# Attention scores in 64x64 tiles without the fully masked blocks, and one chunk's token transposes by DMA

## The chip, the cores and the metric

The kernel runs on one core of one Trainium2 chip. A core has a matrix engine (TensorE, "PE" in the profile; its weight loads are listed apart as "PEld"), VectorE ("DVE"), ScalarE ("ACT"), GpSimd ("POOL"), a queue engine (SyncE, "SP") and 16 DMA engines. The metric is the device time of one execution in microseconds (us); lower is better. A measurement is a median of several runs.

## What is computed

Attention with a sliding window of 128 keys and 4 "sink" keys that every query sees, 4 batches, 8 heads, 768 tokens, 64 numbers a head, and behind it a layer norm and a two-layer network on each token (512 to 2048 to 512), with the attention's output added at the end. Inputs and output are float32; the kernel works in bf16 inside.

```python
scores = (1.0 / np.sqrt(D)) * np.matmul(q, k.transpose(0, 1, 3, 2))
rel = pos[:, None] - pos[None, :]
keep = (pos[None, :] < n_sink) | ((rel >= 0) & (rel < window))     # n_sink 4, window 128
a = softmax(np.where(keep, scores, -1e9))
x = heads_joined(np.matmul(a, v))                                  # 4 x 768 x 512
xn = (x - mean(x)) / np.sqrt(var(x) + 1e-6) * g_ln
out = x + np.maximum(xn @ w_ch1, 0.0) @ w_ch2
```

With blocks of 128 keys and 128 queries, a query block needs two key blocks: its own, of which the half with key not after query is kept, and the one before, of which the half with key after (query − 128) is kept. Each of the two therefore has one 64x64 corner in which nothing is kept.

## The kernel before

**Tiles and chunks.** The 24 tiles of 128 tokens are worked on in 12 chunks of 256 tokens, three to a batch. `R` is a chunk's place in its batch (0, 1, 2). Chunks 0 and 1 have code of their own (`attend_tile`); chunks 2 to 11 go through `attend`. Of these, 2, 4, 5, 7, 8, 10 and 11 have R > 0, so they also use the previous chunk's keys and the sinks; 3, 6 and 9 begin a batch.

**The planner.** Nothing is written out in order by hand. Each piece of work is given to a planner with `P.op(name, engines and assumed durations, due time, function that issues it, buffers read and written)`. The planner (`Plan.run`, L113 to L195) goes through assumed time, places on each engine the ready piece with the lowest due time among those that could start within a short window (0.3 us on TensorE), gives out buffers from rings (L397 to L420; `pair` has two PSUM slots of two banks, `one` four of one bank, `vn` seven, `ot` four), and so fixes the order of instructions on every engine and queue. A `mode` marks which tile shape TensorE uses; a change of mode is assumed to cost `SWITCH`, 0.095 us. From a due time of 40 (`strict`) on, TensorE's pieces are taken in order of due time alone (L129). `PAR` (L229) holds due times and switches. The due times of chunk `c` count from `16c − 8` (`at`, L536); the two-layer network of chunk `c` has due times from `16c + 8`.

**One chunk of `attend`, and lines to know.**

- Loads are issued on GpSimd's queue: L562 (values, `vn`), L575 or L651 (keys and queries). Chunks up to 3 have keys and queries transposed on TensorE (L637), later ones by a DMA transpose on SP's queue (the call is in the helper at L551; started at L652, after the previous chunk's scores).
- Scores, in two halves of four heads: `sc`, L742 to L757. A half has two pair tiles, one for two heads. K is 64, so the array is used as two row tiles, one head in each (`h2`), each with 128 keys as stationary columns. With R > 0 there are three parts of 128, 256 and 128 queries. In the first half the four sink matmuls follow (L756).
- The exponential (L766, ScalarE) and the product with the 0/1 mask (L770, VectorE) run over the whole pair tile, 1024 columns.
- `value` (L782): the sinks' part (L789) and the window's part (L794) on TensorE for each of the two tiles, then reciprocal, product and statistics on VectorE (L807 to L815), a power on GpSimd (L821, L822), the normalised tokens `xc` on VectorE (L824), and their transposition into `xnt` (below).
- The two-layer network, `mlp`: L862 (chunks 0, 1) or L869 (later) is the first layer, evicted at L879; the second layer is L900 for chunks 0 and 1, and for later chunks a scheme with seven products in place of eight at L949 (with L932, L963, L970 on VectorE). The output is stored by SP (L912, L998).

**The transposition of tokens.** It has two forms, and `x_by_dma` says from which chunk on the first is used:

```python
        if c >= PAR["x_by_dma"]:
            P.op(f"trx{t}", {"SP": (1.2, 1.2)}, d + 0.5, lambda e: dma_t(xnt_b[c].t[:, :, 128 * i:128 * i + 128], xc.t),
                 reads=[xc], writes=[xnt_b[c]], dma=HW_X)
            return
        d = at(c, "trx") + 1.0 * i if c >= 2 else d + 0.2
        P.op(f"trx{t}", pe(0.224), d, tr, reads=[xc, Bc["ident"]], writes=[pt],
             hold=[xnt_b[c]])
```

In the second form four transposes on TensorE (L832) write a PSUM bank, and ScalarE or VectorE copies it to `xnt` (the helper's L568 for chunk 2). The first layer of a chunk from 2 on reads both tiles of `xnt` at once.

Of the kernel before, what the change touches and what calls it, by code (L numbers as in the profile page):

```python
# [64 lines left out]
class Plan:  # L65
# [47 lines left out]
    def run(self):  # L113
# [8 lines left out]
        while ready:  # L122
# [5 lines left out]
            for o in ready:  # L128
                if "PE" in o.engs and o is not head and o.prio >= PAR["strict"]:  # L129
                    continue  # L130
# [67 lines left out]
def pe(us):  # L198
    return {"PE": (us, us + Plan.PE_DRAIN)}


def act(n):
    t = 0.065 + 0.000833 * n
    return (t, t + 0.105)


def dve(n, per=1.04):
    t = 0.067 + 0.001 * per * n
    return (t, t + 0.09)


def fix(occ, extra=0.09):
    return (occ, occ + extra)
# [12 lines left out]
NEG = -1e30  # L226
NEVER = -1e9

PAR = dict(strict=40.0, win=0.4, tr=-8.0, sc=-5.3, sc1=-2.0, av=2.0, trx=9.0, by_dma=4, x_by_dma=3, g_on_w=2, behind=5, gtt=9.0, ramp=0.3, vs0=2.6, vpb=12.0,  # L229
           w1p=(0.15, 1.7, 2.05, 2.8), pm=2, w2p=(4.5, 4.51, 4.52, 4.53), by_tile=2, wino=2, vp=(0.0, 0.1, 2.0, 2.1, 4.2, 4.3), ld1=0.05)  # L230


# [129 lines left out]
def kernel(  # L362
# [12 lines left out]
    nc = tc.nc  # L375
# [19 lines left out]
    P = Plan()  # L395
# [56 lines left out]
    def constant(name, eng, us, prio, emit, reads=(), **kw):  # L452
        return P.op(name, {eng: fix(us)}, prio, emit, reads=[Bc[r] for r in reads], **kw)
# [37 lines left out]
    def negs(e):  # L491
# [14 lines left out]
    constant("ones_f", "DVE", 0.06, 7.0, lambda e: V.memset(ones_f, 1.0), writes=[Bc["ones_f"]])  # L506
    constant("masks", "DVE", 0.8, 6.0 if PAR["pm"] == 4 else -20.0, masks, ["upper"], writes=[Bc["mask"]], nb=20.0 if PAR["pm"] == 4 else 0.0)

# [3 lines left out]
    P.op("gtt", pe(0.06), 0.62, lambda e: nc.tensor.transpose(pg.t[:, 0:NDM], g4, ident_f[0:NDM, 0:NDM]),  # L512
         reads=[Bc["g4"], Bc["ident_f"]], writes=[pg], nb=PAR["gtt"])
    P.op("gt", {"DVE": fix(0.08)}, 0.63, lambda e: V.tensor_copy(gt, pg.t[:, 0:NDM]), reads=[pg], writes=[Bc["gt"]])
# [10 lines left out]

    w1prio = PAR["w1p"]
    for c in range(4):
# [3 lines left out]
    for c in range(4):  # L531
        P.op(f"w2ld{c}", {"POOL": (0.75, 0.8)}, PAR["w2p"][c], lambda e, c=c: G.dma_start(
            w2[c], moe_w_ch2[512 * c:512 * (c + 1), :].rearrange("(t p) n -> p t n", p=128)),
            writes=[Bw2[c]], dma=SW_W)

    def at(c, step):  # L536
        return 16.0 * c - 8.0 + PAR[step]

# [5 lines left out]
    tile_of, scores = {}, {}  # L544
# [185 lines left out]
    def attend(c):  # L730
        b, R = c // RC, c % RC
        kq = kq_b[c]
        kprev = kq_b[c - 1] if R else None
        n = 512 if R else 384
        ps, pp_s = (Buf(f"ps{c}", "ps"), Buf(f"pss{c}", "one")) if R else (None, None)
        pes = []
        for half in range(2):
            d = at(c, "sc1" if half else "sc")
            pps = [Buf(f"s{c}{2 * half + i}", "pair") for i in range(2)]
            pbs = [Buf(f"p{c}{2 * half + i}", "pe") for i in range(2)]  # L740

            def sc(e, pps=pps, half=half):  # L742
                if R:
                    parts = [(kprev, 128, 0, 128, 0), (kq, 0, 0, 256, 128), (kq, 128, 128, 256, 384)]
                else:
                    parts = [(kq, 0, 0, 256, 0), (kq, 128, 128, 256, 256)]
                for j, pp in enumerate(pps):
                    hp = 2 * half + j
                    for i, (kt, k0, q0, q1, col) in enumerate(parts):
                        for h2 in range(2):  # L750
                            rs = slice(64 * h2, 64 * h2 + 64)
                            nc.tensor.matmul(pp.t[:, h2, col:col + q1 - q0], lhsT=kt.t[rs, hp, 0, k0:k0 + 128],  # L752
                                             rhs=kq.t[rs, hp, 1, q0:q1], start=i == 0, stop=True, skip_group_check=True)
                if R and half == 0:
                    for hp in range(HP):
                        nc.tensor.matmul(pp_s.t[32 * hp:32 * hp + 32, 0:256], lhsT=kts_b[b].t[:, hp, :],  # L756
                                         rhs=kq.t[:, hp, 1, :], start=True, stop=True, skip_group_check=True)  # L757
            sinks = R and half == 0
            scores[c] = P.op(f"sc{c}{half}", pe(2 * n / 2400 + (0.21 if sinks else 0)), d, sc,
                 reads=[kq] + ([kprev] if R else [])  # L760
                 + ([kts_b[b]] if sinks else []), writes=pps + ([pp_s] if sinks else []),
                 hold=pbs + ([ps] if sinks else []), mode=("r", "c") if sinks else "r")
            for j, pp in enumerate(pps):
                hp = 2 * half + j
                pb = pbs[j]
                P.op(f"ex{c}{hp}", {"ACT": act(2 * n)}, d + 0.1 + 0.05 * j, lambda e, pp=pp, pb=pb: nc.scalar.activation(  # L766
                    pb.t[:, :, 0:n], pp.t[:, :, 0:n], AF.Exp, scale=scale), reads=[pp], writes=[pb])
                mm = (mask if R else mask0).rearrange("p a b c -> p a (b c)")
                P.op(f"mk{c}{hp}", {"DVE": dve(2 * n, 0.52)}, d + 0.2 + 0.05 * j, lambda e, pb=pb, mm=mm:
                     V.tensor_mul(pb.t[:, :, 0:n], pb.t[:, :, 0:n], mm),  # L770
                     reads=[Bc["mask" if R else "mask0"]], rw=[pb])
                pes.append(pb)
            if sinks:
                P.op(f"sx{c}", {"ACT": act(256)}, d + 0.6, lambda e: nc.scalar.activation(
                    ps.t, pp_s.t[:, 0:256], AF.Exp, scale=scale), reads=[pp_s], writes=[ps])
        for i in range(2):
            def part(h, n, i=i):
                col = 256 * i + 128 * n if R else 128 * (i + n)
                return pes[h // 2].t[:, h % 2, col:col + 128]
            value(c, i, pes, ps, at(c, "av") + 1.0 * i, part, [2 * c + i - 1, 2 * c + i] if R or i else [2 * c])  # L780

    def value(c, i, pes, ps, d, part, srcs):  # L782
        b, R, t = c // RC, c % RC, 2 * c + i
# [218 lines left out]
    for c in range(NC):  # L1002
        chunk(c)
        if c < 2:
            if c:
                first_sinks()
            attend_tile(2 * c)
            attend_tile(2 * c + 1)
        else:
            attend(c)  # L1010
# [34 lines left out]
    for o in order:  # L1045
# [7 lines left out]
        if free and left > 0.11:  # L1053
            i, nth = min(free)[1], 0
# [55 lines left out]
```

## Time and profile before

| | us |
|---|---|
| median of 3 runs | 215.95 (215.31 to 216.34) |
| the profiled execution | 215.84 |
| its span, first to last instruction | 214.3 |
| granted TensorE clock | 0.994 of full |

A few groups from the list of costliest ones (busy us; mean ns of one):

| line, engine | what | count | busy | mean |
|---|---|---|---|---|
| L869 PE | first layer, 128x256 | 640 | 74.5 | 273 |
| L752 PE | scores, 64x256 of 64*128 tiles | 80 | 9.6 | 271 |
| L752 PE | scores, 64x128 of 64*128 tiles | 80 and 56 | 8.4 and 6.3 | 216 and 221 |
| L756 PE | sinks, 128*32 tiles | 28 | 2.0 | 283 |
| L794 PE | values, 128x65 | 352 | 14.6 | 193 |
| L832 PE | token transposes | 24 | 2.3 | 220 |
| L766 ACT | exponential, 1024 columns | 28 | 27.1 | 1023 |
| L770 DVE | mask product, 1024 columns | 28 | 18.6 | 683 |
| L551 SPq | DMA transposes into `kq` / `xnt` | 32 / 18 | | 1228 / 1190 (median, issue) |

How to read it: a span is cut into 40 slices of 5.36 us, and a digit is the busy share in tenths. "Busy" of a group joins overlapping instructions. In a timeline a line is "start, length, engine, line, operation, out<-in, shape, count"; neighbours of one kind are merged, and brackets tell idle time before it with what ended it. The chain of waits goes back from the last instruction, at each step to what released it.

### The profile page before, as it was taken

How to read it: one execution, taken by the hardware profiler on the slowest of the kernel's cores; microseconds unless marked ns; L12 is line 12 of the kernel's file. 1: busy time of each engine (PE TensorE's matmuls, PEld its weight loads, DVE VectorE, ACT ScalarE, POOL GpSimd, SP SyncE). 2: the span in 40 equal slices, each digit the busy share in tenths (PEclk: the TensorE clock that was granted, in tenths of full speed). 3: DMA queues.
4: the chain of work that ended last, by engine and by line, in shares of the span. 5: the costliest groups of instructions: out<-in, count | busy, mean ns of one | idle time of the engine just before them, and what ended most of it. 6: DMA issues, size and time to landing. Idle time of an engine off the chain costs nothing.

```text
span 214.3 us, 5912 instructions
## 1 busy us (share of the span) xinstructions
PE 205.9 (96%) x2375; PEld 168.3 (79%) x2381; DVE 162.2 (76%) x408; ACT 115.3 (54%) x173; POOL 83.7 (39%) x126
## 2 busy tenths in 40 slices
PE   6999999999999999999999999999999999999990
PEld 2568995683787987987987987988988988988880
DVE  5689769898587688697786796797787777794470
ACT  2488579457565555554457357355555555532600
POOL 7966583449057066066075174174110110110000
PEclk9999999999999999999999999999999999999997
DMA  6999999999979939929969939939931520222003
GB/s 111 154 198 187 198 191 207 186 199 131 170 129 134 164 96 125 213 62 133 165 110 158 196 50 157 193 46 161 191 75 38 140 49 11 90 49 90 13 22 91
DMA packets 99914, 27.23 MB, mean 127 GB/s; under 512 B 88356, under 2 KB 97064, under 8 KB 99880
## 3 DMA queue, kind: packets, MB, share of 16 engines
q0 software_dynamic: 67712, 13.37, 78.5%
q1 hardware_dynamic: 31640, 13.15, 31.8%
q8 instruction: 20, 0.33, 0.7%
q10 hardware_dynamic: 528, 0.26, 0.5%
q14 instruction: 14, 0.11, 0.2%
HBM read 27.30 MB, written 6.29 MB: 157 GB/s over the span
## 4 chain that ended last, share of the span: by engine, by line
PE 83%; DMA 7%; POOL 5%; DVE 2%; issue 1%; DVEq 0%
PE one L869 33%; PE one L949 29%; DMA w<-in_moe_w_ch_dram 7%; PE one L900 6%; PE pair L752 5%; PE pair L794 4%; PE one L862 3%; POOL vn L562 2%; PE pair L789 1%; POOL nat L597 1%; PE one L756 1%; POOL st L822 1%; POOL n4b L575 1%; DVE st L813 1%; PE one L637 0%
## 5 line engine op out<-in xcount | busy, mean ns | idle before, releaser
L879 ACT ACTIVATE hq<-one 128x512 bf16<-128x512 f32 x94 | 56.1, 599 | 56.3 <-PE one L869 46.9
L869 PE MATMUL one<-xnt,w 128*128 128x256 bf16 x640 | 74.5, 273 | 0.0
L869 PEld LDWEIGHTS <-w 128*128 128x128 bf16 x640 | 61.4, 98 | 7.0
L766 ACT ACTIVATE pe<-pair 128x1024 bf16<-128x1024 f32 (+1 forms) x40 | 36.2, 960 | 23.9 <-PE pair L752 23.9
L821 POOL TENSOR_SCALAR st<-st 128x1 f32<-128x1 f32 x24 | 6.3, 262 | 88.2 <-DVE rec L807 74.0
L949 PEld LDWEIGHTS <-hs 128*128 128x128 bf16 x320 | 30.0, 98 | 5.6 <-issue 1.3
L963 DVE TENSOR_TENSOR tm<-one,x 128x256 f32<-128x256 f32 x40 | 16.9, 422 | 13.4 <-PE one L949 13.4
L770 DVE TENSOR_TENSOR pe<-pe,mask 128x1024 bf16<-128x1024 bf16 (+1 forms) x40 | 25.0, 643 | 1.6 <-ACT pe L766 1.4
L949 PEld LDWEIGHTS <-hq 128*128 128x128 bf16 x240 | 23.4, 98 | 2.7
L562 POOL DMA_DIRECT2D vn<-in_v_dram x24 | 21.8, 922 | 3.0 <-DMA w<-in_moe_w_ch_dram 1.6
L932 DVE TENSOR_TENSOR hs<-hq 128x512 bf16<-128x512 bf16 x40 | 15.4, 413 | 5.1 <-ACT hq L879 5.1
L949 PE MATMUL one<-w,hq 128*128 128x256 bf16 x160 | 19.1, 273 | 0.0
L970 DVE TENSOR_TENSOR ot<-one,tm 128x256 f32<-128x256 f32 x40 | 16.7, 417 | 1.3 <-PE one L949 1.1
L809 DVE TENSOR_TENSOR x<-pair,rec 128x512 bf16<-128x512 f32 x24 | 16.6, 691 | 0.8
L813 DVE BATCH_NORM_STATS2 st<-x 128x6 f32<-128x512 bf16 x24 | 16.6, 691 | 0.4
L862 PE MATMUL one<-xnt,w 128*128 128x128 bf16 x256 | 15.9, 219 | 0.2 <-DMA w<-in_moe_w_ch_dram 0.2
L651 POOL DMA_DIRECT2D nat<-in_k_dram x16 | 14.9, 930 | 2.4 <-DMA w<-in_moe_w_ch_dram 2.4
L651 POOL DMA_DIRECT2D nat<-in_q_dram x16 | 14.1, 896 | 3.9 <-DMA w<-in_moe_w_ch_dram 3.9
L862 PEld LDWEIGHTS <-w 128*128 128x128 bf16 x256 | 14.5, 98 | 1.0 <-DMA w<-in_moe_w_ch_dram 0.3
L822 POOL TENSOR_TENSOR st<-st,mhalf 128x1 f32<-128x1 f32 x24 | 14.5, 604 | 2.0
L900 PE MATMUL one<-w,hq 128*128 128x512 bf16 x60 | 15.0, 380 | 0.2
L794 PE MATMUL pair<-vn,pe 128*128 128x65 bf16 x352 | 14.6, 193 | 0.0
(113 smaller groups left out, 249.4 us busy)
## 6 DMA issues: line engine op xcount, KB each, us to landing
out_dram<-ot SPq DMA_DIRECT2D x22, 256.0 KB
w<-in_moe_w_ch_dram POOLq DMA_DIRECT2D x8, 512.0 KB, 12.8
vn<-in_v_dram POOLq DMA_DIRECT2D x24, 128.0 KB, 7.1
nat<-in_k_dram POOLq DMA_DIRECT2D x17, 128.0 KB, 5.1
nat<-in_q_dram POOLq DMA_DIRECT2D x17, 128.0 KB, 6.3
kq<-nat SPq DMA_TRANSPOSE x32
out_dram<-ot SPq DMA_DIRECT2D x4, 128.0 KB
xnt<-xc SPq DMA_TRANSPOSE x18
```

What stands on the lines that cost most here:

```text
L562: P.op(f"vld{t}", {"POOL": (0.87, 0.9)}, prio, lambda e: G.dma_start(bv.t[:, :, 0:64], v[b, :, 128 * r:128 * (r + 1), :].rearrange("h p d ...
L651: lambda e, nat=nat, ap=ap: G.dma_start(nat.t, ap), writes=[nat], dma=SW, after=behind(c))
L766: P.op(f"ex{c}{hp}", {"ACT": act(2 * n)}, d + 0.1 + 0.05 * j, lambda e, pp=pp, pb=pb: nc.scalar.activation(pb.t[:, :, 0:n], pp.t[:, :, 0:n ...
L770: V.tensor_mul(pb.t[:, :, 0:n], pb.t[:, :, 0:n], mm),
L794: nc.tensor.matmul(po.t[:, h // 4, 65 * (h % 4):65 * (h % 4) + 65], lhsT=part(h, n), rhs=vn_b[tv].t[:, h, :], start=(not R and h % 4 == 0 ...
L813: P.op(f"bn{t}", {"DVE": fix(0.60)}, d + 0.12, lambda e: V.bn_stats(st.t[:, 8:14], x.t), reads=[x], writes=[st, mv])
L862: nc.tensor.matmul(ph.t[:, 128 * s:128 * s + 128], lhsT=w1[u // 2][:, j, 128 * s:128 * s + 128], rhs=xnt.t[:, j, 128 * (u % 2):128 * (u % ...
L869: nc.tensor.matmul(ph.t[:, 256 * s:256 * s + 256], lhsT=w1[ht // 4][:, j, 128 * (ht % 4):128 * (ht % 4 + 1)], rhs=xnt.t[:, j, :], start=j ...
L879: nc.scalar.activation(hg.t[:, u % 4, :], ph.t, AF.Relu)
L900: nc.tensor.matmul(pc.t[:, 0:wd], lhsT=(hq[s // 2].t[:, (2 * s + i) % 4, 128 * ii:128 * ii + 128] if by_tile else hq[ht // 8].t[:, ht // 2 ...
L949: nc.tensor.matmul(at(r), lhsT=get(left, g)[:, v, s, :], rhs=rhs, start=first and n == 0, stop=n == 7, skip_group_check=True)
L963: return P.op(f"tm{name}_{c}", {"DVE": dve(256, 1.14)}, pr, lambda e: V.tensor_tensor(tm[name].t, at(r), xs[i].t[:, sl], op=ALU.add), read ...
```

## The change

1. `sc` with R > 0: each matmul is split over the key columns into two of 64 (`m`), so that a stationary operand is 64x64 and four tiles are in use (two heads by two halves of the keys). `cut` gives for each part and each half of the keys the query columns that are computed: of the previous block the first 64 keys meet only the first 64 queries, and so on. The 64x64 blocks that the mask clears entirely are not written; the exponential and the mask product still run over all columns, with what the slot held before in those blocks. A half has 24 matmuls instead of 12.
2. The planner's assumed duration of such a half falls from 2·512 to 2·384 columns, and it is marked with a mode of its own, "q".
3. `x_by_dma` 3 becomes 2: chunk 2's tokens go by DMA transposes.
4. The due time of `value` for chunk 2 goes from 26 and 27 to 20 and 21 (`av2`; `avi`, 1.0, stands for the constant that was there).

```diff
-PAR = dict(strict=40.0, win=0.4, tr=-8.0, sc=-5.3, sc1=-2.0, av=2.0, trx=9.0, by_dma=4, x_by_dma=3, g_on_w=2, behind=5, gtt=9.0, ramp=0.3, vs0=2.6, vpb=12.0,
+PAR = dict(strict=40.0, win=0.4, tr=-8.0, sc=-5.3, sc1=-2.0, av=2.0, trx=9.0, by_dma=4, x_by_dma=2, g_on_w=2, av2=20.0, avi=1.0, behind=5, gtt=9.0, ramp=0.3, vs0=2.6, vpb=12.0,
...
                     parts = [(kprev, 128, 0, 128, 0), (kq, 0, 0, 256, 128), (kq, 128, 128, 256, 384)]
+                    cut = [((0, 64), (0, 128)), ((0, 192), (64, 256)), ((0, 128), (64, 128))]
...
-                        for h2 in range(2):
-                            rs = slice(64 * h2, 64 * h2 + 64)
-                            nc.tensor.matmul(pp.t[:, h2, col:col + q1 - q0], lhsT=kt.t[rs, hp, 0, k0:k0 + 128],
-                                             rhs=kq.t[rs, hp, 1, q0:q1], start=i == 0, stop=True, skip_group_check=True)
+                        for m in range(2 if R else 1):
+                            n0, n1 = (cut[i][m] if R else (0, q1 - q0))
+                            for h2 in range(2):
+                                rs, ks = slice(64 * h2, 64 * h2 + 64), slice(64 * m, 64 * m + 64) if R else slice(0, 128)
+                                nc.tensor.matmul(pp.t[ks, h2, col + n0:col + n1], lhsT=kt.t[rs, hp, 0, k0 + ks.start:k0 + ks.stop],
+                                                 rhs=kq.t[rs, hp, 1, q0 + n0:q0 + n1], start=i == 0, stop=True, skip_group_check=True)
...
-            scores[c] = P.op(f"sc{c}{half}", pe(2 * n / 2400 + (0.21 if sinks else 0)), d, sc,
+            scores[c] = P.op(f"sc{c}{half}", pe(2 * (384 if R else n) / 2400 + (0.21 if sinks else 0)), d, sc,
...
-                 hold=pbs + ([ps] if sinks else []), mode=("r", "c") if sinks else "r")
+                 hold=pbs + ([ps] if sinks else []), mode=("q", "c") if sinks else "q" if R else "r")
...
-            value(c, i, pes, ps, at(c, "av") + 1.0 * i, part, [2 * c + i - 1, 2 * c + i] if R or i else [2 * c])
+            value(c, i, pes, ps, (PAR["av2"] if c == 2 else at(c, "av")) + PAR["avi"] * i, part, [2 * c + i - 1, 2 * c + i] if R or i else [2 * c])
```

## The prediction

> **What bounds the kernel now.** I read the page first (busy time, the slices), then the chain of waits, then TensorE's timeline around the stages that the change touches, then the shapes, last the DMA transposes.
>
> ```profile
> PE 205.9 (96%) x2375; PEld 168.3 (79%) x2381; DVE 162.2 (76%) x408; ACT 115.3 (54%) x173; POOL 83.7 (39%) x126
> PE   6999999999999999999999999999999999999990
> DMA  6999999999979939929969939939931520222003
> ```
>
> TensorE is busy in tenths of 9 from the second slice to the last but one; no other engine is. The DMA engines are as full up to about 60 us, and from then on have gaps (slices of 3 and 2), so loads catch up. The chain of waits says the same: weights from DMA until 26 us, then TensorE, with one detour over VectorE and GpSimd that ends in `xc` and L832:
>
> ```profile
> 10.91 15.07 DMA w<-in_moe_w_ch_dram
> ...
> 48.57 0.42 DVE xc L824
> 49.04 0.40 PE one L832 x4
> ...
> 65.17 0.55 PE pair L752 x12
> ```
>
> So a microsecond of TensorE's own time saved after 26 us is a microsecond of the end, unless a new wait eats it. The two pieces to price are the score stage (L752) and the transposes of chunk 2 (L832). TensorE's timeline of both, with two stages that serve as rows below:
>
> ```profile
> 45.50 1.08 PE L637 MATMUL one<-ident,n4a 128*64 128x128 bf16 x32
> ...
> 47.39 0.39 PE L832 MATMUL one<-ident,xc 128*128 128x128 bf16 x4
> 47.61 1.03 PE L900 MATMUL one<-w,hq 128*128 128x512 bf16 x4
> 49.04 0.40 PE L832 MATMUL one<-ident,xc 128*128 128x128 bf16 x4 [0.40 <-DVE xc L824]
> ...
> 65.11 0.23 PE L752 MATMUL pair<-kq,kq 64*128 64x128 bf16 x2
> 65.17 0.33 PE L752 MATMUL pair<-kq 64*128 64x256 bf16 x4
> 65.34 0.22 PE L752 MATMUL pair<-kq,kq 64*128 64x128 bf16 x2
> 65.39 0.33 PE L752 MATMUL pair<-kq 64*128 64x256 bf16 x4
> 65.65 0.29 PE L756 MATMUL one<-kq,kts 128*32 128x256 bf16 x4
> ...
> 72.88 0.65 PE L794 MATMUL pair<-vn,pe 128*128 128x65 bf16 x16
> ```
>
> The first number is the start. A matmul's duration holds its drain, which lies beside the next matmul; what counts is the distance of starts.
>
> **Scores (14 half-chunks: chunks 2, 4, 5, 7, 8, 10, 11, two halves each).** Now: 12 matmuls in a half, two row tiles at once, each streaming 128+256+128 = 512 columns for each of two pair tiles. The second pair tile starts 65.34 − 65.11 = 0.23 us after the first, and the sink matmuls start 0.31 after that, 0.09 of it the switch to another tile shape (the same 0.1 lies before 65.11: the last matmul there starts at 64.90 and streams 0.11). So a pair tile is 0.22 us, 0.43 ns a column. After: 24 matmuls of 64x64, four tiles at once, each tile 64+192+128 or 128+192+64 = 384 columns. At 0.43 ns that is 0.165 us a pair tile; the upper bound of the gain is 0.055 a pair tile, 0.11 a half, 14 × 0.11 = 1.54 us.
>
> What the trace doesn't show is a 64x64 tile, and how long its weight load holds up a matmul of only 64 columns (28 ns). The nearest rows are the matmuls of L637 and L794 above, and their weight loads among the shapes (busy us, mean ns):
>
> ```profile
> L794 PEld LDWEIGHTS <-pe 128*128 128x128 bf16 x352 | 13.8, 97 | 0.8
> ...
> L637 PEld LDWEIGHTS <-n4a 128*64 128x64 bf16 x32 | 0.9, 110 | 0.1
> ```
>
> L637 runs two column tiles with loads of 64 columns: 32 matmuls in 1.08 − 0.22 (one drain) = 0.86 us, 27 ns each, so 54–55 a tile for 128 columns at 0.43 ns (55). The load is hidden, hence at most 54 ns. L794 is the short one: 16 matmuls of 65 columns in 0.65 − 0.19 = 0.46 us, 31 ns where streaming needs 28: its load of 128 columns takes at most 31. The 64-column load of L637 is recorded 110 − 97 = 13 ns longer, so I take 31 + 12 = 43 ns, nearer to L637 because its shape is. Then each pair tile has one matmul of 64 columns in each column half that lasts 43 instead of 28: 0.165 + 0.015 = 0.18 us. Gain 0.04 a pair tile, 0.08 a half; the first load of a stage is bare and 110 − 94 = 16 ns longer than now (L752's loads have a mean of 94), which leaves 0.065. 14 × 0.065 = **0.9 us**. With loads of 54 ns it is 14 × (2 × 0.029 − 0.016) = 0.6; with hidden ones 1.5; if loads don't hide at all, a loss (rivals). The Trainium skill (TensorEngine Tiling (Array Packing), Restrictions and Gotchas) says column tiling switches the fast weight load off, and TensorE: Matmul & The Clock Gate (LDWEIGHTS) puts a load's ns at its columns divided by 1.2, an estimate of 53 ns for 64. By that figure the scores would give 0.6 us; L637's 54 ns agrees with it and can't tell it from mine.
>
> The number of switches stays: row tiles, in the first half then column tiles for the sinks, become 64x64 tiles, then column tiles. The exponentials and mask products (L766 at 1023 ns, L770 at 683 ns) still run over 1024 columns, the unwritten blocks too, so ScalarE and VectorE gain nothing.
>
> **Transposes of chunk 2.** Removed from TensorE: two groups of four at L832, each 0.22 us of starts (47.39 to 47.61, 49.04 to 49.27), 0.44 together. Also gone is the second group's wait: the four L900 before it start at 47.61 and take 4 × 0.216 = 0.86, so TensorE could have gone on at 48.47 and did at 49.04: 0.57 us lost. Sum **1.0 us**. ScalarE loses two evictions of 0.59 us (L568, 48.6 and 50.3), off the path.
>
> Added: two DMA transposes on SP's queue, 1.19 us each to issue, in front of the store at 52.5 and the key/query transposes from 53.0; SP does nothing between 44.4 and 52.5, so this costs nothing while they are issued there. Their landing I take from the semaphore events: the sixteenth comes 2.4 to 6.6 us after the issue, 6.6 for the one at 53.0 us, when the DMA engines are full as they are here. If `xc` of the second tile came at 48.99 as now, the landing would be 55.6, and the first-layer matmuls (L869, now 55.54, then about 54.4) would wait 1.2 us.
>
> That is what moving `value` of chunk 2 covers. Its two stages (L789 and L794) start at 40.48 and 42.91. Their last operand, the fourth masked tile, is ready at 39.05 (L770). With the lower due time they go in when the running group of L900 ends, about 39.6 and 40.3, 2.6 us earlier for the second tile. Behind them move VectorE's L807 to L824 and GpSimd's L821/L822 (GpSimd's queue then is loads that wait for the DMA's turn, up to 2.2 us), giving `xc` near 46.4 and a landing by 53.0: 1.4 us of slack. The work passed over (the rest of chunks 0 and 1) is later by 1.4 us, and so are stores, for which nothing waits with four `ot` buffers; TensorE's sum is the same. Two more transposes are at most 1.4 us each of all DMA engines (q1's 31.8% of 214.3 us over its fifty transposes, its stores counted in), so the next keys and queries (last landing 62.9, needed at 65.1) come up to 2.8 us later on full engines, with 2.2 of cover; part of it goes into the gaps before 65 us, and I charge nothing.
>
> **Sum.** −0.9 − 1.0 = −1.9 us against the profiled execution's 215.84 (span 214.3): 213.9. The median of the runs, 215.95, is 0.1 above that execution, so I forecast **214.0**, span 212.4.
>
> **Rivals.**
> Scores give nothing. If four tiles get no further than two, because loads of 54 ns and bare first loads add up, only the transposes pay: 214.9. For it: no 64x64 row; against: two-way packing works both by rows and by columns. 0.12.
>
> Tokens late. DMA contention or a blocked GpSimd queue holds `xc` or its landing, and the first layer of chunk 2, or the scores of chunk 4, wait up to 1.2 us: 215.2. For it: the longest landing is 6.6 us and slack 1.4. 0.10.
>
> Slower: loads don't lie beside matmuls of the same rows. Its place is L752, where two column tiles share each row half. Then each of the three rounds of a pair tile costs its longest matmul plus a load: 55 + 82 + 55 + 3 × 43 = 321 ns against 220; +0.2 a half, 14 × 0.2 = +2.8, less 1.0: 217.7. It decides from 9 ns of bare load a round, where a pair tile is back at 220 (192 + 3 × 9); from 21 ns the 28 pair tiles cost the 1.0 us of the transposes as well. Against it: L637's tiles share all rows and would need 55 + 43 = 98 ns, not 54. 0.09. The Trainium skill's page TensorE: Matmul & The Clock Gate (Packing small matmuls, The mechanism) states just this, that a load overlaps only matmuls of another row group. L637 disagrees, at 27 ns a matmul.
>
> Slower: instruction rate. The fastest long row hands out a load and a matmul every 27 ns (L637); the new stage wants 24 pairs in 0.34 us, 14 ns each. Bound at 27 it takes 0.65 instead of 0.44: +2.9 − 1.0, 217.9. Against: L756's four start within 0.29 − 0.283 = 7 ns of each other, and the long matmuls before let instructions queue up. 0.07.
>
> **Numbers.** The forecast has 0.62, mostly 213.3 to 214.6. The range 213.2 to 216.0 takes in the hidden-load bound, nothing from scores, and late tokens; it leaves out the two slower ones. A measurement here tells about 0.5% (1.08 us) from no change. Faster than 214.87: nearly all of the forecast, half of the first rival, a little of the second: 0.68. Within: 0.16. Slower: 0.16.
>
> **What would show it.** L752 with 64*64 tiles, 24 starts in about 0.37 us (chain pieces of 0.47 instead of 0.55; 0.55 or more means a slower rival); L832 x16, no wait on `xc` on TensorE; 20 transposes into `xnt`; the first L869 near 54.4. I am wrong if that L869 has a wait on DMA before it, if L752's loads show gaps, or if TensorE stalls between 40 and 50 us for banks that late evictions hold.

## The result, and the profile after

The changed kernel takes 213.95 us (median of 11 runs, 213.37 to 214.69); the kernel before, run beside it, 215.64 (11 runs, 215.15 to 216.36). The ratio is 0.9914, 95% interval 0.9897 to 0.9932: 1.7 us faster by the medians, 1.5 to 2.2 by the interval, beyond the 0.5% that such a measurement can tell. The forecast was 214.0. The profiled execution took 213.8 with a span of 212.2, where 212.4 was expected.

All lines of the new kernel from the score stage on are three higher (L752 is L755, L869 is L872). The page of the kernel after, busy times and slices:

```profile
PE 204.2 (96%) x2535; PEld 168.1 (79%) x2541; DVE 161.6 (76%) x408; ACT 114.5 (54%) x171; POOL 83.4 (39%) x126
PE   6999999999999999999999999999999999999990
DMA  5999999999999959939979959969934421122002
```

TensorE has 160 matmuls more (168 of the scores, less 8 transposes) and is busy 1.7 us less; ScalarE has two evictions less. TensorE is still what bounds the kernel. The chain of waits of the kernel after, in the stretch where the detour over `xc` was (start, length, work):

```profile
49.05 0.44 PE pair L755 x8
49.49 2.70 PE one L903 x12
52.18 0.44 PE pair L755 x8
52.62 1.83 PE one L903 x8
54.45 1.75 PE one L872 x16
...
63.93 0.46 PE pair L755 x24
64.39 0.22 PE one L759 x4
```

There is no step over VectorE or GpSimd left between 44 and 54 us, and a half of the scores is 0.46 where it was 0.55. TensorE's timeline of the same kernel, and two lines of SP's queue:

```profile
39.38 0.39 PE L792 MATMUL pair<-vs,ps 128*128 128x260 bf16 x2
...
40.09 0.39 PE L792 MATMUL pair<-vs,ps 128*128 128x260 bf16 x2
...
63.86 0.25 PE L755 MATMUL pair<-kq,kq 64*64 64x64 bf16 x4
63.91 0.31 PE L755 MATMUL pair<-kq 64*64 64x192 bf16 x8
64.05 0.23 PE L755 MATMUL pair<-kq,kq 64*64 64x64 bf16 x4
64.08 0.31 PE L755 MATMUL pair<-kq 64*64 64x192 bf16 x8
64.32 0.29 PE L759 MATMUL one<-kq,kts 128*32 128x256 bf16 x4
```

```profile
43.68 0.38 SPq L915 DMA_DIRECT2D out_dram<-ot  x1
44.18 3.43 SPq L551 DMA_TRANSPOSE xnt<-xc  x2
```

What to see: `value` of chunk 2 went in at 39.38 and 40.09 (40.48 and 42.91 before). A pair tile of scores lasts 64.05 − 63.86 = 0.19 us, the second 64.32 − 64.05 − 0.09 (the switch) = 0.18; by the same reading they were 0.23 and 0.22. The two token transposes are issued at 44.18 and 46.41 and land, by the semaphore events, at 52.06 and 53.33; the first L872 starts at 54.29.

### The profile page after: what moved, and what is told of

Its sections match the earlier page's. It is cut to its first block, busy times and chain, and to the rows that moved or that the text cites. A ratio compares the mean times of both kernels' runs of the same rounds, so it can differ in the third digit from the quotient of the medians.

```text
span 212.2 us, 6233 instructions
## 1 busy us (share of the span) xinstructions
PE 204.2 (96%) x2535; PEld 168.1 (79%) x2541; DVE 161.6 (76%) x408; ACT 114.5 (54%) x171; POOL 83.4 (39%) x126
## 4 chain that ended last, share of the span: by engine, by line
PE 95%; DVE 2%; issue 0%; DVEq 0%
PE one L872 33%; PE one L952 30%; PE one L865 7%; PE one L903 7%; PE pair L797 5%; PE pair L755 4%; PE pair L792 2%; PE one L1069 2%; PE one L637 2%; PE pair L1069 1%; PE pair L693 1%; PE one L759 1%; PE pair L705 1%; PE one L835 1%; DVE st L816 0%
## 5 line engine op out<-in xcount | busy, mean ns | idle before, releaser
L872 PE MATMUL one<-xnt,w 128*128 128x256 bf16 x640 | 74.5, 273 | 0.0
L872 PEld LDWEIGHTS <-w 128*128 128x128 bf16 x640 | 61.4, 98 | 7.1
```

Of the source, the lines that this page charges most:

```text
L872: nc.tensor.matmul(ph.t[:, 256 * s:256 * s + 256], lhsT=w1[ht // 4][:, j, 128 * (ht % 4):128 * (ht % 4 + 1)], rhs=xnt.t[:, j, :], start=j ...
```

## The experiments

Two figures are given for each kernel. One is the time with its ratio to the kernel before, run beside it. The other comes from the one profiled execution: the stretch from TensorE's first score matmul of chunk 2 (32.02 us in the kernel after) to the first one of chunk 11's second half (176.50). That first matmul lies anywhere from 31.6 to 33.0 us in the fourteen traces, whatever the kernel, a spread of over half of what the change gains. In the three latest (again, full_columns, pieces_of_64) the chain of waits lies on the weights' loads until about 27 us. The stretch leaves this out. It holds 13 of the 14 halves.

| kernel | median us | ratio (95%) | stretch us | against before |
|---|---|---|---|---|
| before | 215.64 to 215.85 | 1 | 146.62 | |
| after | 213.95 | 0.9914 (0.9897–0.9932) | 144.48 | −2.14 |
| again (after) | 213.95 | 0.9919 (0.9897–0.9940) | 144.48 | −2.14 |
| scores_only | 214.89 | 0.9953 (0.9934–0.9972) | 145.49 | −1.13 |
| tokens_only | 215.13 | 0.9969 (0.9953–0.9986) | 145.61 | −1.01 |
| move_only | 214.97 | 0.9958 (0.9943–0.9973) | 146.05 | −0.57 |
| scores_move | 213.92 | 0.9920 (0.9899–0.9941) | 144.93 | −1.69 |
| no_move | 213.80 | 0.9902 (0.9885–0.9919) | 144.75 | −1.87 |
| full_columns | 215.05 | 0.9963 (0.9948–0.9979) | 145.84 | −0.78 |
| pieces_of_64 | 215.12 | 0.9969 (0.9946–0.9992) | 145.56 | −1.06 |
| eighths | 214.25 | 0.9931 (0.9906–0.9957) | 145.13 | −1.49 |
| loads_held | 214.13 | 0.9927 (0.9907–0.9947) | 144.48 | −2.14 |
| loads_held_no_move | 213.61 | 0.9900 (0.9878–0.9921) | 144.48 | −2.14 |
| loads_behind_next | 214.80 | 0.9952 (0.9933–0.9971) | 145.79 | −0.83 |

> The changed kernel as it is, once more, beside the next three on the same chip: 213.95, ratio 0.991. Its transposes of chunk 2's second tile land 0.5 to 1 us before the first L872 can start, or after it: in the traces of three other kernels with the same tokens (no_move, pieces_of_64, eighths) that L872 waited 0.26, 0.43 and 0.56 us, in three more it didn't.

Time and ratio came out the same, and two executions of the changed kernel have the same stretch to 0.01 us. So differences of 0.1 in it are read here, though each stretch is that of one execution; the times tell apart some 0.4. (The second transpose landed at 54.27 in this one, 0.8 us before the first L872.)

### Which part brings what

```diff
 scores_only (to after)
-x_by_dma=2   av2=20.0
+x_by_dma=3   av2=26.0
```

> Only the score stage is changed (64x64 tiles, blocks left out); tokens of chunk 2 by TensorE and the old due times, as before. Theory A (TensorE's starts add up): each of the 14 halves goes from 0.545/0.548 us to 0.462/0.464, 14 x 0.083 = 1.17 us, so 215.64 - 1.17 = 214.5 (ratio 0.9946), and the wait of about 0.57 us on xc before the second L832 group stays. Rival B (the gain of the whole is the tokens' and the planner's new order; scores give nothing at the end): 215.6.

Stretch −1.13, time 214.89, and the halves take 0.462 and 0.464 us to the next start, each 0.083 less than before. Rival B falls. The wait that theory A said would stay is there (TensorE's timeline of scores_only):

```profile
48.57 0.40 PE L835 MATMUL one<-ident,xc 128*128 128x128 bf16 x4 [0.39 <-DVE xc L827]
```

```diff
 tokens_only (to before)
-x_by_dma=3   ... at(c, "av") + 1.0 * i
+x_by_dma=2   ... (20.0 if c == 2 else at(c, "av")) + 1.0 * i
```

> Old score stage; chunk 2's tokens by DMA and its values at the earlier due time. Theory A: 0.44 us of transposes and 0.57 of wait are gone from TensorE, the first L869 starts about 54.5 us instead of 55.54, 215.64 - 1.0 = 214.6 (ratio 0.9953). With scores_only it must add up to the whole, 1.17 + 1.0 = 2.2. Rival B: 214.0, all of the gain is here. Rival C (part of the gain needs both): 215.1 or more.

Stretch −1.01, as theory A has it, and −1.13 − 1.01 = −2.14 is the whole: in the stretches the parts add up, and neither needs the other. The first L869 started at 54.27. The time, 215.13 (−0.3 to −1.0 by its interval), lies at the weak end and is as a number what rival C named. But by the ratios the two parts bring −1.0 and −0.7 us and the whole −1.9, each to about ±0.4, so the times don't show that anything is missing.

```diff
 move_only (to before)
-at(c, "av") + 1.0 * i
+(20.0 if c == 2 else at(c, "av")) + 1.0 * i
```

> Old score stage, tokens by TensorE as before; only the due time of chunk 2's values is lowered to 20 and 21. Theory A: xc of the second tile is ready some 2.5 us earlier, so the wait of 0.57 us before the second L832 group is gone, 215.64 - 0.57 = 215.1, and the 0.44 of the transposes stays. Rival: the wait is only exchanged for another one behind the passed-over evictions, 215.6.

Stretch −0.57: the earlier due time alone takes the wait away, and between this stretch and that of tokens_only the transposes on TensorE are the other 0.44. The second group of transposes no longer has idle time before it:

```profile
48.20 0.39 PE L832 MATMUL one<-ident,xc 128*128 128x128 bf16 x4
```

The times don't show the 0.44: 214.97 here, 215.13 with the DMA transposes too.

### Was the earlier due time needed?

```diff
 no_move (to after)
-av2=20.0
+av2=26.0
```

> The changed kernel with the old due times (26 and 27) for chunk 2's values. Theory A: xc of the second tile is ready near 48.6 us and its DMA transpose lands 6 to 8 us later, 55 to 56.5, while the first L872 could start at 54.3: it waits 0.7 to 2 us, 213.95 + 0.7 to 2 = 214.7 to 216. Rival (landing isn't the limit, the move was not needed): no wait before that L872, 213.95.

A miss for theory A's size, and the time is the rival's. The second transpose was issued at 49.32 and landed at 54.66, 5.3 us later, and the first L872 started at 54.71, by starts 0.26 us late; the time is no worse than the changed kernel's. Issued 2.9 us earlier, the transpose lands only 1.3 us earlier (53.33). So the landing doesn't follow the issue. The next kernels ask what the early due time is worth, and whether it is DMA traffic that holds the landing.

```diff
 scores_move (to after)
-x_by_dma=2
+x_by_dma=3
```

> New score stage and the earlier due time, but chunk 2's tokens by TensorE. Theory A (TensorE's starts add up): 0.44 us of transposes are back and no wait, so 213.95 + 0.44 = 214.4. Theory H (in many executions the first L872 waits for the DMA transposes about as long as those on TensorE take): the same as the changed kernel, 213.95, within 0.15.

Stretch 144.93, 0.45 more than after, as theory A has it; the times, 213.92 and 213.95, say theory H. Both can be: in the traces of eighths and pieces_of_64 the first L872 waited. The list of waits of eighths has it:

```profile
PE one L872 <- DMA xnt<-xc: 0.4, 1, 0.4
```

By starts that is 0.56 us, in pieces_of_64 0.43, with landings at 54.70 and 55.47. How often this happens in unprofiled executions wasn't measured, and 0.45 us is at the edge of what the times tell, so whether the DMA transposes beat those on TensorE in the mean stays open.

The four kernels with the new scores show it together. The ratios are 0.9953 with neither step for chunk 2 (scores_only), 0.9920 with the earlier due time alone (scores_move), 0.9902 with the DMA transposes alone (no_move) and 0.9914 with both (after). Either step by itself brings 0.7 or 1.1 us, each to about ±0.5. What the second adds to the first, 0.27 or 0.45 in the stretches, no time shows.

```diff
 loads_held (to after); loads_held_no_move: the same with av2=26.0
-        return [roots[2 * (c - 3) + 1]] if c >= PAR["behind"] else []
+        return [trx[5]] if c == 5 else [roots[2 * (c - 3) + 1]] if c >= PAR["behind"] else []
...
-            P.op(f"trx{t}", {"SP": (1.2, 1.2)}, ...
+            trx[t] = P.op(f"trx{t}", {"SP": (1.2, 1.2)}, ...
```

> The changed kernel, with the loads of chunk 5 held back until the DMA transpose of chunk 2's second tile has landed (they were held until that tile's power on GpSimd, 1 us before the transpose is issued, and go out between 45.9 and 51.3 us). Theory H (the landing is set by the loads that share the DMA engines): the second transpose, issued near 46.4, lands by 51.5 instead of 53.3 to 55.5, the first L872 never waits, 213.95 - 0.1 to 0.3 = 213.7. Rival I (older backlog sets it, or the held loads come too late for chunk 5): landing as before, 213.95, or a stall at chunk 5's scores near 80 us and 214.5 or more.

> As loads_held, with the old due times (26 and 27) for chunk 2's values. Theory H: issued near 49.3, the second transpose lands about 2.5 to 4 us later, 52 to 53.5, before the first L872 at 54.4: no wait, and the early due time is worth nothing: 213.7. Rival I (backlog older than chunk 5's loads): landing at 54.7 or later and a wait of 0.3 us or more, 214.1.

Neither decides. The edit reached the planner only: the planned order sets no wait on a landing, and in loads_held GpSimd still issued chunk 5's loads from 45.49 us, right behind the power, as before. Landing at 52.82 and, without the move, 54.06; no L872 waited, and both times are the changed kernel's within their intervals. So a last kernel held the loads by GpSimd's own order:

```diff
 loads_behind_next (to after)
-        return [roots[2 * (c - 3) + 1]] if c >= PAR["behind"] else []
+        return [roots[6 if c == 5 else 2 * (c - 3) + 1]] if c >= PAR["behind"] else []
```

> The changed kernel, with chunk 5's loads placed behind chunk 3's first power on GpSimd (58.5 us) in place of chunk 2's second (45.4 us). GpSimd works in order, so this holds them in fact, where loads_held only moved them in the plan and they still went out at 45.5. Theory H (these loads set the landing of chunk 2's DMA transposes): the second transpose, issued near 46.4, lands by 51 instead of 52.8 to 55.5; first L872 without a wait; time 213.95 - 0 to 0.3. Rival I (work issued before 46 us sets it): landing 53 or later as before. Danger: chunk 5's keys and queries come late for its scores at 79.7, then TensorE waits there and the time is 214.5 or more.

GpSimd's timeline and TensorE's waits of that kernel:

```profile
44.99 0.57 POOL L825 TENSOR_TENSOR st<-st,mhalf 128x1 f32<-128x1 f32 x1
...
58.92 1.88 POOL L651 DMA_DIRECT2D nat<-in_k_dram  x2
```

```profile
PE pair L755 <- DMA kq<-nat: 1.1, 1, 1.1
```

Now the loads are held, and the second transpose (issued 46.04) lands at 51.64, 2.3 us before the first L872 (53.92) in place of 1.0. That is 5.6 us after its issue, against 6.8 to 8.3 in the seven other traces with DMA transposes and the earlier due time: as far as one trace shows, chunk 5's loads do delay it. But the first one (issued 43.81) lands at 51.31, 7.5 us later, hardly sooner than the 7.9 of the changed kernel, so these loads aren't what holds that one. Theory H is half right.

The packets in the traces point at the store that SP issues 0.5 us before the first transpose. In the changed kernel its packets (2 KB each, on the same DMA queue) start from 45.67 to 48.32 us, and those of the two transposes (256 bytes each) from 47.52 to 52.60. In loads_behind_next it is 45.13 to 47.76, then 47.17 to 51.01. The transpose that the kernel before issues at 187.01, with no packet left on that queue, has its first one 1.17 us after the issue, where the changed kernel's needs 3.3. No run moves the store, so its share beside that of the older loads stays open.

The price is the stated danger: chunk 5's scores near 80 us wait for their keys and queries, 1.30 us by starts, and the kernel is slower than the changed one.

### What the four tiles do

```diff
 full_columns (to after)
-cut = [((0, 64), (0, 128)), ((0, 192), (64, 256)), ((0, 128), (64, 128))]
+cut = [((0, 128), (0, 128)), ((0, 256), (0, 256)), ((0, 128), (0, 128))]
...
-... pe(2 * (384 if R else n) / 2400 ...
+... pe(2 * n / 2400 ...
```

> The changed kernel with 64x64 tiles, but no block left out: each of the four tiles streams all 512 columns of a pair tile. Theory A (the gain is the columns; four tiles at once are worth nothing by themselves): a half takes what it took before plus 0.01 to 0.02 us of a longer first load, about 0.56 us; 213.95 + 14 x 0.098 = 215.3. Rival D (smaller tiles are faster by themselves): a half near 0.46, 214.0.

TensorE's timeline of a half in full_columns:

```profile
68.61 0.25 PE L755 MATMUL pair<-kq,kq 64*64 64x128 bf16 x4
...
68.85 0.23 PE L755 MATMUL pair<-kq,kq 64*64 64x128 bf16 x4
...
69.18 0.39 PE L952 MATMUL one<-n4b,hs 128*128 128x256 bf16 x2
```

A half is 0.57 us, 0.02 more than with row tiles (0.548). Four tiles at once gain nothing by themselves; the gain is the columns left out. Rival D falls.

```diff
 pieces_of_64 (to after)
-for m in range(2 if R else 1): ...
+jobs = [(m, a0, a0 + 64) for m in range(2) for a0 in range(*cut[i][m], 64)]   # by a0 - cut[i][m][0], then m
```

> The changed kernel with each score matmul cut into pieces of 64 queries, each with its own weight load: the same columns in 48 pairs of load and matmul instead of 24. Theory A (a load of 64 columns hides wholly behind a matmul of 64, and pairs are handed out faster than one in 7 ns): only 2.5 ns more for each matmul added, a half about 0.48 us, 214.2. Rival E (a load takes 43 ns, as I predicted, so a piece takes 43 instead of 29): 12 x 43 = 0.52 and the switch, a half about 0.63, 14 x 0.17 = +2.4, 216.3. Rival F (a pair every 14 ns at best): 48 x 14 = 0.67, a half 0.78, 218.4.

TensorE's timeline of a half in pieces_of_64:

```profile
68.55 0.22 PE L755 MATMUL pair<-kq,kq 64*64 64x64 bf16 x4
68.60 0.20 PE L755 MATMUL pair<-kq 64*64 64x64 bf16 x2
...
68.76 0.20 PE L755 MATMUL pair<-kq,kq 64*64 64x64 bf16 x4
```

From the second piece of the first pair tile (68.60) to the first of the next (68.76) are five pieces, 0.032 us each, where streaming 64 columns needs 0.028. So a load of 64 columns takes at most 32 ns of a tile's time, and it lies beside matmuls, on tiles of which two share each half of the rows. A half is 0.513, nearer to theory A's 0.48 than to E's 0.63 or F's 0.78; 48 pairs of load and matmul were handed out in some 0.4 us, 8 ns each (the four of a piece mostly start 3 ns apart, then comes a pause of 22). The stretch grew by 1.08, of which 13 × 0.05 = 0.65 are the scores and 0.43 the wait on chunk 2's tokens told above. In eighths, next, that wait is 0.56 of the 0.65 by which the stretch is longer than the changed kernel's.

```diff
 eighths (to after)
-for m in range(2 if R else 1):   ... slice(64 * m, 64 * m + 64)
+for m in range(4 if R else 1):   ... slice(32 * m, 32 * m + 32)
-cut = [((0, 64), (0, 128)), ((0, 192), (64, 256)), ((0, 128), (64, 128))]
+cut = [[(0, 32 * m + 32) for m in range(4)], [(32 * m, 160 + 32 * m) for m in range(4)], [(32 * m, 128) for m in range(4)]]
...
-... pe(2 * (384 if R else n) / 2400 ...
+... pe(2 * (320 if R else n) / 2400 ...
```

> Eight tiles of 64x32 (two heads by four quarters of the keys), leaving out what the mask clears entirely at 32 keys: 320 columns a tile and pair tile instead of 384, 48 matmuls a half, the shortest of 32 queries. Theory A (columns, 0.43 ns each, and 2.5 ns a matmul): 28 x 64 x 0.43 = 0.77 us less at best, and a first load half as long; a half about 0.40, 213.95 - 0.8 = 213.1. Rival G (a matmul has a floor near 28 ns, so 32 queries cost as much as 64): 28 x (0.028 - 0.014) less, 213.55. Rival E (loads of narrow tiles don't hide): a half at or over 0.46, 213.95 or more.

TensorE's timeline of a half in eighths:

```profile
67.74 0.25 PE L755 MATMUL pair<-kq,kq 64*32 64x32 bf16 x8
...
67.90 0.18 PE L755 MATMUL pair<-kq 64*32 64x32 bf16 x1
...
68.21 0.61 PE L952 MATMUL one<-n4b,hs 128*128 128x256 bf16 x4
```

Not faster: a half is 0.468 us where the changed kernel has 0.464, which is the size that rival E named. The first pair tile gains, 0.16 instead of 0.19; the second gives it back, 68.21 − 67.90 − 0.09 = 0.22 instead of 0.18. That speaks against a floor or unhidden loads, which would hit both alike, and would fit a supply of instructions that runs short: 24 pairs in a 0.137 us pair tile are 5.7 ns each, and the second pair tile's 24 came in 0.20, 8 to 9 ns each. The 8 ns of pieces_of_64 doesn't confirm such a limit, since there the starts within a piece come 3 ns apart. No run separates this from another cause that sets in late.

## Why the prediction was right

**What bounds.** TensorE was right: by starts the scores take 13 × 0.084 = 1.09 us less of it and the tokens 0.44 + 0.57 = 1.01, 2.10 together, and the stretch is 2.14 shorter. The two parts, each tried alone, add up to the whole within 0.01.

**The number.** That 213.95 lies 0.05 from the forecast is in part luck. The forecast counted from 215.95, and beside the changed kernel the kernel before took 215.64. The forecast gain of 1.9 lies between the 1.7 of the medians (1.5 to 2.2) and the 2.2 that the traces add up to (14 × 0.083 + 1.01). No run shows whether these two really differ, and if so why.

**Scores.** The mechanism held and the size was too small: 14 × 0.083 = 1.2 us, against 0.9. The term that was off is the weight load behind a matmul of 64 columns, put at 43 ns: the 31 of L794 and 12 of the 13 ns by which L637's loads are recorded longer. It is at most 32 (pieces_of_64), so a short matmul loses at most 4 ns and not 15. The changed kernel's own timeline agrees: in the second pair tile the next matmuls follow those of 64 columns after 64.08 − 64.05 = 0.03 us, and streaming needs 0.028. The bare first load was right: by starts the first pair tile of a half is 24 ns longer than the second, 10 ns before; 16 ns more were assumed.

**Transposes.** 0.44 and 0.57 were priced, and 0.44 and 0.57 measured in the stretches (tokens_only, move_only). Of the 0.44 the times show nothing, as told above. Nothing was charged for the next keys and queries, and in the changed kernel rightly so: the last of them lands at 62.73, and the scores use it at 63.86 without a wait.

**The move.** Its places were right to 0.3 us (39.6 and 40.3 forecast, 39.38 and 40.09 measured; the landing by 53.0, 53.33 measured), its worth was not: without it 1.2 us of waiting were forecast, and 0.26 came, as the transpose landed 5.3 us after its issue and not 6.6. The slack was misread too. The longest landing in the trace of the kernel before isn't 6.6 us but 7.4 (a key/query transpose issued at 81.87 landed at 89.31), and chunk 2's two took 7.9 and 6.9, so the slack was 1.0 and not 1.4, and in eighths and pieces_of_64 there was none. Its use with transposes on TensorE, where it alone is worth 0.57, the prediction didn't mention.

**Rivals.** "Scores give nothing" fell with scores_only. "Loads don't lie beside matmuls of the same rows" fell with the 64x64 rows themselves: 321 ns a pair tile were priced, 170 to 194 measured by starts. The Trainium skill's rule that stood beside it, that a load overlaps only matmuls of another row group (TensorE: Matmul & The Clock Gate, Packing small matmuls, The mechanism), disagrees with these runs too. The estimate of 53 ns for a load of 64 columns, by the Trainium skill's same page (LDWEIGHTS), doesn't agree either: 32 is the bound here. "Instruction rate" was priced at 27 ns a pair; pairs came at 8. "Tokens late" is real in part: three of the ten traces with DMA transposes for chunk 2 show waits of 0.26 to 0.56 us, two of them with the earlier due time, though not the profiled execution of the changed kernel.

## What to carry to other kernels

Where TensorE bounds the kernel, count streamed columns: splitting the array into smaller tiles paid here by the blocks that could then be left out and by nothing else, and the next split, into more and shorter matmuls, no longer paid. Compare traces over a stretch that begins behind a varying load phase; differences of 0.1 us are seen there that medians of ten runs don't tell. But a trace is one execution: a gain that no median shows isn't yet a gain in the mean. A transpose moved to DMA is free only while its landing has cover, and on full DMA engines an earlier issue bought less than it moved (2.9 us earlier, landed 1.3 earlier).

## What was not expected

- A load and matmul of 64 columns on one of four 64x64 tiles: 32 ns, four at once, from 48 pairs in 0.4 us.
- As far as the times tell, either of the two steps for chunk 2, the earlier due time or the DMA transposes, brings alone what both bring.
- With eight 64x32 tiles, 320 columns took as long as 384 on four tiles (0.468 and 0.464 us a half).
- DMA transposes of one 128x512 bf16 tile landed 4.8 to 9.3 us after their issue in the stretch from 43 to 55 us, the later issue mostly the sooner (no_move: 49.32 to 54.66; pieces_of_64: 44.98 to 54.25).
- Taking chunk 5's loads out of that stretch brought the second landing from 6.9 to 5.6 us after issue, and cost 1.30 us at chunk 5.
